# The last 320 columns of wo group 4 in fifteen short transfers instead of with the rest

## The chip, the cores and the metric

The kernel runs on one core of a Trainium2 chip. The metric is device time in microseconds (us) of one execution; three executions of the kernel before gave 526.68, 526.82 and 527.18 us, so its time is 526.82 us, the median. The core has five engines that work side by side and meet through semaphores: PE (TensorE, matmuls), DVE (VectorE), ACT (ScalarE), POOL (GpSimd) and SP (SyncE). Here SP does nothing but issue DMA transfers, and 16 DMA engines move what it issues.

## The reference: what is computed

Four tokens (batch 4, one position each, D = 640) are normalised, and two branches are added to them: attention over a cache, and a gated feed-forward layer.

```python
W = min(4096, max(256, Sk // 4))                 # 2048 of the 8192 cached positions
q = (xn @ wq).reshape(4, 1, 32, 192)             # 32 heads of 192
scores = einsum("bhqd,bhkd->bhqk", q, k[:, :, Sk - W:]) * 192 ** -0.5
p = softmax(scores)
o = einsum("bhqk,bhkd->bhqd", p, v[:, :, Sk - W:])
return x + o.reshape(4, 1, 6144) @ wo + (silu(xn @ w1) * (xn @ w3)) @ w2
```

Every head has keys and values of its own, so each element of the windows of K and V is used for one token only. Of the 222.96 MB that are read, nearly all is K and V: 32 heads with two tensors of 3 MB each.

## The kernel before

**Tiling.** A head's K window, 4 tokens by 2048 positions by 192, lies in SBUF as 128 partitions by 64 positions by 192 (24,576 bytes in each partition); V lies in the same way. There are two K buffers (`kt`) and two V buffers (`vt`). The vector `q` is spread over all partitions (`qbc`).

**One head.** DVE multiplies K by q in two halves (`mult`, L275, 128x6144 each). For each half PE adds the products in groups through an identity matrix (`adder`, L373, 12 matmuls), and DVE reduces what is left (`reduce_half`, L281). Then comes the softmax: a maximum (L286), a transpose on PE (`tr`, L431), a second maximum (L290), ACT's scaling (L352), PE's broadcast (`bc`, L435), ACT's exponential (L356) and the masked weights `z` (L295). PE multiplies them with V (`pv`, L448). Two heads share a normalisation (`osum`, L456, and L299, L304); a transpose (L307) makes `oT`, one for each group of four heads.

**The output projection.** `wo` has 6144 rows, taken as eight groups of 768 rows (`hg` 0 to 7). A group lies as 128 partitions by 6 rows by 640, so 3840 elements, or 7680 bytes, in a partition. The matmuls of a group (`proj`, L385) run late: groups 0 to 4 among the last heads, and groups 5 to 7 behind the last head.

**The order of SP's queue** is written out by hand. First come wq, w1, w3 and w2; then for each head `load_k` and `load_v`. `load_k(h+2)` waits until DVE's reduction has shown that the K buffer is free (`s_red`, L158), and `load_v` until PE has finished with the V buffer (`s_pv`, L164). The w1, w3 and w2 tiles (`wts[0]` to `wts[2]`) are free early, and three issues at L188 put wo into them: groups 0 and 1 at h = 4, groups 2 and 3 at h = 6, and group 4 alone at h = 8, each after `load_k(h+2)` and `load_v(h+1)`. All three count up one semaphore, `s_wom`, by 16 each. PE waits for 48 on it (L498) ahead of `proj(0)`. Groups 5, 6 and 7 go into a K buffer at the very end (L196, L198, L199).

**Parts that matter for the change:** `wo_of(hg)` and `wo_src(hg)` (L145 to L151) give a group's place in SBUF and its source, both with 128 rows of 3840 elements; SP's loop (L180 to L189); and PE's wait (L498).

Of the kernel before, what the change touches and what calls it, by code (L numbers as in the profile page):

```python
# [16 lines left out]
def kernel(  # L17
# [14 lines left out]
    P = 128  # L32
    B, Sq, D = A_x.shape
# [16 lines left out]
    QW = HG * Dh  # L50
    RPP = QW // P
    N0 = D // 2
    QC = 512
    NQ = H * Dh // QC
    FW = F // HG
    NP = H // 2
    assert D % P == 0 and F % QC == 0 and P % B == 0 and W % (PB * GQ) == 0
    assert JQ * DD == 512 and JQ % 2 == 0 and 2 * Dh + 2 <= 512 and 2 * N0 == D and N0 <= 512
    assert NQ == 12 and KC == 5 and QW % P == 0 and Dh == CT * RPP and P == HG * CT and F == HG * CT * FC
# [11 lines left out]
    def sb(name, shape, dt):  # L71
        return ctx.enter_context(nc.sbuf_tensor(name, shape, dt))
# [9 lines left out]
    wts = [sb(f"wt{i}", [P, KC * F], BF16) for i in range(3)]  # L82
# [62 lines left out]
    def wo_of(hg):  # L145
        t = wts[hg // 2][:, :] if hg < 5 else wo_end
        i = hg % 2 if hg < 5 else hg - 5
        return t[:, i * RPP * D:(i + 1) * RPP * D]

    def wo_src(hg):  # L150
        return A_wo[hg * QW:(hg + 1) * QW, :].rearrange("(p i) n -> p (i n)", i=RPP)  # L151


    sp = nc.sync

    def load_k(h):
        if h >= 2:
            sp.wait_ge(s_red, 2 * (h - 2) + 1)  # L158
        sp.dma_start(out=flat(kt[h % 2]), in_=k_win[:, h].rearrange("b (p j) d -> p b (j d)", p=PB)).then_inc(s_k[h % 2], 16)

    def load_v(h, j0=0, j1=NJ, s=None):
        if j0 == 0:
            if h >= 2:
                sp.wait_ge(s_pv, h - 1)  # L164
            else:
                sp.wait_ge(s_pp, 13)
        sp.dma_start(out=vt[h % 2][:, j0:j1, :].rearrange("q j d -> q (j d)"),
                     in_=v_win[:, h].rearrange("b (p j) d -> p b j d", p=PB)[:, :, j0:j1, :].rearrange("p b j d -> p b (j d)")
                     ).then_inc(s or s_v[h % 2], 16)
# [10 lines left out]
    for h in range(H - 2):  # L180
        load_k(h + 2)
        if h < H - 4:
            load_v(h + 1)
        if h in (4, 6, 8):
            g = h - 4
            n = 2 if g < 4 else 1
            sp.wait_ge(s_pp, 16)
            sp.dma_start(out=wts[g // 2][:, 0:n * RPP * D].rearrange("p (g i) -> p g i", g=n),  # L188
                         in_=A_wo[g * QW:(g + n) * QW, :].rearrange("(g p i) n -> p g (i n)", g=n, i=RPP)).then_inc(s_wom, 16)  # L189
    load_v(H - 3)  # L190
    load_v(H - 2)
    load_v(H - 1, 0, NJ // 2)
# [38 lines left out]
    def dv(fn, *a, own=True, **k):  # L231
        if n_dv[0] and own:
            ve.wait_ge(s_dv, n_dv[0])
        fn(*a, **k).then_inc(s_dv, 1)  # L234
        n_dv[0] += 1
        return n_dv[0]
# [22 lines left out]
    for c0 in (0, 6):  # L259
        for i in (1, 3, 5):  # L260
            ve.wait_ge(s_pp, 1 + c0 + i + 1)
            n = dv(ve.tensor_copy, out=qbc[:, (c0 + i) * QC:(c0 + i + 1) * QC], in_=q_banks[i], own=False)
# [35 lines left out]
    def norm_rec():  # L298
        ve.reciprocal(out=rt[:], in_=mt[:, P + 1:P + 2]).then_inc(s_rec, 1)  # L299

    def norm_og(i):
        sl = slice(i % 2 * 2 * CT, (i % 2 + 1) * 2 * CT)
        ve.wait_ge(s_sum, 2 * i + 2)
        ve.tensor_scalar_mul(out=og[sl].rearrange("p i r -> p (i r)"), in0=po[sl, 0:Dh], scalar1=rt[sl, 0:1]).then_inc(s_og, 1)  # L304
        if i % 2:
            ve.wait_ge(s_og, i + 1)
            ve.transpose(out=oT[:, i // 2].rearrange("p i r -> p (i r)"), in_=flat(og)).then_inc(s_oT, 1)  # L307
# [23 lines left out]
    norm_rec()  # L331
    ve.wait_ge(s_rec, NP)
    norm_og(NP - 1)
    ve.wait_ge(s_acc, 1)  # L334
# [35 lines left out]
    pe = nc.tensor  # L370
# [67 lines left out]
    def tot():  # L438
        for par in range(2):
            m = pe.matmul(mt[:, P + 1:P + 2], lhsT=flat(tot_w[:, par]), rhs=rsum[par][:], start=(par == 0), stop=(par == 1))  # L440
        return m
# [35 lines left out]
    pe.addr_align(256, max_nops=8)  # L477
    with pe.While(lambda: pe.snap(cnt) < NP - 1):
        for par in range(2):
# [15 lines left out]
    adder(1)  # L495
    take(pe, s_z)
    tot()
    pe.wait_ge(s_wom, 48)  # L498
    pe.wait_ge(s_oT, 5)
    proj(0)  # L500
    pv(1)
# [60 lines left out]
```

## Time and profile before

| | |
|---|---|
| three runs | 526.68, 526.82, 527.18 us |
| the profiled execution's own time | 526.78 us |
| its span, first to last instruction | 524.9 us |
| busy PE, DVE, ACT | 366.4, 334.6, 54.1 us |
| mean granted TensorE clock | 0.857 |
| moved by DMA | 223.07 MB, mean 425 GB/s |
| issues of K | 32 of 3072 KB, median 19.6 us from issue to landing |
| issues of V | 31 of 3072 KB, 22.5 us; 2 of 1536 KB, 10.8 us |
| issues of wo into `wts` | 2 of 1920 KB, 28.6 us; 1 of 960 KB (group 4), 29.1 us |

The page divides the span into 40 slices of 13.1 us and gives for each one the busy share of every engine, the granted clock and the traffic. The trace behind it can be asked for the instructions of a stretch in order of time, for who waited for whom, and for the packets that the DMA engines moved. A packet record has its queue, start, duration and size; queue q1 is SP's, q10 is ACT's, and the two queues of the kind "instruction" fetch the engines' programs.

### The profile page before, as it was taken

The page shows a single profiled execution, that of the slowest core. Times are in us where ns is not written, and L with a number is a line of the kernel's source. Part 1 is how long each engine was busy: PE and PEld are TensorE (multiplying, and loading weights), DVE is VectorE, ACT ScalarE, POOL GpSimd, SP SyncE. Part 2 cuts the span into 40 slices and gives each one's busy share as a digit, 9 for nine tenths or more (in the row PEclk, how much of TensorE's full clock was granted, in tenths as well). Part 3 has the DMA queues.
Part 4 walks back from the last instruction along what each step waited for, and adds up shares of the span by engine and source line. Part 5 has one row for each costly group of instructions (what it writes and reads, how often), then busy time and mean ns, then how long its engine had stood idle before and what let it go on. Part 6 is the DMA issues. An engine that isn't in the chain of part 4 may idle for free. (4 is left out here: it accounts for less than half of the span.)

```text
span 524.9 us, 4774 instructions
## 1 busy us (share of the span) xinstructions
PE 366.4 (70%) x2306; PEld 83.7 (16%) x1553; DVE 334.6 (64%) x287; ACT 54.1 (10%) x174; POOL 3.4 (1%) x16
## 2 busy tenths in 40 slices
PE   2775777667586367876667666887676767587897
PEld 0010111111211011121111111111111112111133
DVE  3136777767267564678767676667776666666871
ACT  2120101101101011011101111110110011111010
POOL 2000000000000000000000000000000000000000
PEclk9887888878869788788878888888797888888799
DMA  8999999999999999999999999999999999999995
GB/s 356 423 441 429 428 436 426 442 421 427 443 429 436 427 427 444 429 431 438 425 440 425 438 429 433 434 429 438 425 442 423 440 429 431 438 425 440 425 424 231
DMA packets 11520, 223.07 MB, mean 425 GB/s; under 512 B 1260, under 2 KB 1400, under 8 KB 2424
## 3 DMA queue, kind: packets, MB, share of 16 engines
q1 hardware_dynamic: 11496, 222.96, 98.9%
q8 instruction: 4, 0.07, 0.0%
q14 instruction: 4, 0.03, 0.0%
q10 hardware_dynamic: 16, 0.01, 0.0%
HBM read 222.96 MB, written 0.01 MB: 425 GB/s over the span
## 5 line engine op out<-in xcount | busy, mean ns | idle before, releaser
L373 PE MATMUL ps<-prs,idb 128*128 128x512 bf16 x768 | 229.0, 461 | 134.1 <-PEq L136 134.1
L275 DVE TENSOR_TENSOR prs<-kt,qbc 128x6144 bf16<-128x6144 bf16 x64 | 214.5, 3353 | 120.1 <-DMA kt<-in_A_k_cache_dram 120.1
L281 DVE TENSOR_REDUCE sc<-ps 128x32 f32<-128x1024 f32 x64 | 77.5, 1211 | 3.3 <-PE ps L373 3.1
L456 PE MATMUL po<-o_sb,sel_w 128*128 128x192 f32 x128 | 49.0, 516 | 0.7 <-PEq L136 0.7
L448 PE MATMUL o_ps<-vt,z 128*8 128x384 bf16 x1024 | 47.2, 326 | 0.1
L352 ACT ACTIVATE gneg<-gmax 1x128 f32<-1x128 f32 x32 | 9.8, 308 | 290.1 <-DVE gmax L290 290.1
L448 PEld LDWEIGHTS o_ps<-vt,z 128*8 128x8 bf16 x1024 | 22.1, 86 | 54.6 <-issue 42.0
L422 PEld LDWEIGHTS <-idb 128*128 128x128 bf16 x64 | 6.3, 98 | 153.1 <-issue 152.6
L456 PEld LDWEIGHTS po<-o_sb,sel_w 128*128 128x128 f32 x128 | 25.3, 221 | 14.7 <-issue 5.2
L359 ACT COPY o_sb<-o_ps 128x384 f32<-128x384 f32 x32 | 15.3, 479 | 117.4 <-PE o_ps L448 117.4
L295 DVE TENSOR_TENSOR z<-ex,mask_b 128x256 bf16<-128x256 bf16 x32 | 13.6, 424 | 18.9 <-ACT ex L356 18.4
L431 PEld LDWEIGHTS mt<-idf,lmax 128*1 128x1 f32 x32 | 3.3, 104 | 118.9 <-issue 118.9
L290 DVE TENSOR_REDUCE gmax<-mt 1x4 f32<-1x128 f32 x32 | 8.8, 276 | 10.6 <-PE mt L431 10.1
L440 PEld LDWEIGHTS mt<-rsum,tot_w 128*128 128x128 f32 x64 | 9.6, 191 | 35.1 <-issue 34.7
L234 DVE CAST qbc<-ps 128x512 bf16<-128x512 f32 x4 | 2.6, 686 | 19.7 <-PE ps L373 19.7
L435 PE MATMUL mt<-one,gneg 1*128 1x1 f32 x64 | 11.9, 253 | 4.0 <-PEq L136 3.8
L373 PE MATMUL ps<-vt,xnT 128*128 128x512 bf16 x31 | 10.6, 477 | 5.0 <-DMA vt<-in_A_wq_dram 3.9
L435 PEld LDWEIGHTS mt<-one,gneg 1*128 1x128 f32 x64 | 9.4, 182 | 22.4 <-issue 22.4
L356 ACT ACTIVATE ex<-sc,negm 128x64 bf16<-128x64 f32 x32 | 11.1, 348 | 1.0
L431 PE MATMUL mt<-idf,lmax 128*1 128x128 f32 x32 | 10.5, 328 | 0.0
L304 DVE TENSOR_SCALAR og<-po,rt 64x192 bf16<-64x192 f32 x16 | 6.6, 414 | 3.8 <-PE po L456 3.6
L440 PE MATMUL mt<-rsum,tot_w 128*128 128x1 f32 x64 | 8.1, 231 | 0.0
(65 smaller groups left out, 79.6 us busy)
## 6 DMA issues: line engine op xcount, KB each, us to landing
kt<-in_A_k_cache_dram SPq DMA_DIRECT2D x32, 3072.0 KB, 19.6
vt<-in_A_v_cache_dram SPq DMA_DIRECT2D x31, 3072.0 KB, 22.5
vt<-in_A_wq_dram SPq DMA_DIRECT2D x2, 3072.0 KB, 13.2
wt<-in_B_w_dram SPq DMA_DIRECT2D x3, 1920.0 KB, 27.8
wt<-in_A_wo_dram SPq DMA_DIRECT2D x2, 1920.0 KB, 28.6
vt<-in_A_v_cache_dram SPq DMA_DIRECT2D x2, 1536.0 KB, 10.8
kt<-in_A_wo_dram SPq DMA_DIRECT2D x2, 960.0 KB, 14.6
prs<-in_A_wq_dram SPq DMA_DIRECT2D x1, 1536.0 KB, 19.9
```

What stands on the lines that cost most here:

```text
L275: ve.tensor_tensor(out=prs[:, a].rearrange("p q j d -> p (q j) d"), in0=kt[h % 2][:, 2 * a * JQ:2 * (a + 1) * JQ, :], in1=qbc[:, h * Dh:(h ...
L281: ve.tensor_reduce(out=sc[h % 3][:, 2 * a * JQ:2 * (a + 1) * JQ], in_=ps[:, a].rearrange("p q (j d) -> p (q j) d", d=DD), axis=AX.X, op=AL ...
L295: ve.tensor_tensor(out=z[h % 2][:], in0=ex[h % 2][:].unsqueeze(2).to_broadcast([P, NJ, B]), in1=mask_b[:].unsqueeze(1).to_broadcast([P, NJ ...
L352: ae.mul(out=gneg[h % 2][:], in_=gmax[h % 2][:].unsqueeze(1).to_broadcast([1, PB, B]), mul=-SCALE).then_inc(s_gneg, 1)
L356: ae.activation(out=ex[h % 2][:], in_=sc[h % 3][:], func=ACTF.Exp, bias=negm[h % 2][:, 0:1], scale=SCALE, accum_out=rsum[h % 2][:]).then_i ...
L359: ae.copy(out=o_sb[h % 2][:], in_=o_ps[:, 0:2 * Dh]).then_inc(s_osb, 1)
L373: return pe.add_instruction(mybir.InstMatmult(name=nc.get_next_instruction_name(), engine=pe.engine, ins=[pe.lower_ap(rhs), pe.lower_ap(lh ...
L431: pe.transpose(out=mt[0:1, 0:P], in_=lmax[par][:], identity=idf[:]).then_inc(s_tr, 1)
L435: pe.matmul(mt[:, P:P + 1], lhsT=flat(gneg[par]), rhs=one[:], start=True, stop=True).then_inc(s_bc, 1)
L440: m = pe.matmul(mt[:, P + 1:P + 2], lhsT=flat(tot_w[:, par]), rhs=rsum[par][:], start=(par == 0), stop=(par == 1))
L448: m = pe.matmul(o_ps[c * CT:c * CT + 2 * B, 0:2 * Dh].rearrange("p (a d) -> p a d", a=2), lhsT=z[par][:, 2 * jj:2 * jj + 2, :], rhs=vt[par ...
L456: m = pe.matmul(po[:, 0:Dh], lhsT=flat(sel_w[:, par, k]), rhs=o_sb[par][:, k * Dh:(k + 1) * Dh].rearrange("p (r i) -> p i r", i=RPP), star ...
```

## The change

The transfers of groups 0 to 3 stay as they are. Group 4's transfer of 128 rows by 3840 elements becomes one of 128 rows by the first 3520 elements (7040 bytes a row), and after it 15 transfers of the last 320 elements (640 bytes a row): rows 0 to 14, then rows 15 to 28, and so on with 13, 12, ..., 2 rows, and 9 rows at the end (together 128). Each adds 16 to `s_wom`, and PE waits for 48 + 16 x 15 = 288 in place of 48. The bytes and their places are the same.

```diff
+    CUTS = [*range(15, 1, -1), 9]
+    assert sum(CUTS) == P
...
             sp.wait_ge(s_pp, 16)
-            sp.dma_start(out=wts[g // 2][:, 0:n * RPP * D].rearrange("p (g i) -> p g i", g=n),
-                         in_=A_wo[g * QW:(g + n) * QW, :].rearrange("(g p i) n -> p g (i n)", g=n, i=RPP)).then_inc(s_wom, 16)
+            if n == 2:
+                sp.dma_start(out=wts[g // 2][:, 0:n * RPP * D].rearrange("p (g i) -> p g i", g=n),
+                             in_=A_wo[g * QW:(g + n) * QW, :].rearrange("(g p i) n -> p g (i n)", g=n, i=RPP)).then_inc(s_wom, 16)
+            else:
+                c1 = RPP * D - N0
+                sp.dma_start(out=wo_of(g)[:, 0:c1], in_=wo_src(g)[:, 0:c1]).then_inc(s_wom, 16)
+                r0 = 0
+                for r in CUTS:
+                    sp.dma_start(out=wo_of(g)[r0:r0 + r, c1:], in_=wo_src(g)[r0:r0 + r, c1:]).then_inc(s_wom, 16)
+                    r0 += r
...
-    pe.wait_ge(s_wom, 48)
+    pe.wait_ge(s_wom, 48 + 16 * len(CUTS))
```

## The prediction

> **What bounds the kernel now.** I read the page's slices and queues first, then the waits of the last 45 us, then the instructions of that stretch in order of time, and last the packet records.
>
> The page, slices and queues:
>
> ```profile
> DVE  3136777767267564678767676667776666666871
> DMA  8999999999999999999999999999999999999995
> GB/s 356 423 441 429 428 436 426 442 421 427 443 429 436 427 427 444 429 431 438 425 440 425 438 429 433 434 429 438 425 442 423 440 429 431 438 425 440 425 424 231
> q1 hardware_dynamic: 11496, 222.96, 98.9%
> q8 instruction: 4, 0.07, 0.0%
> q14 instruction: 4, 0.03, 0.0%
> ```
>
> The DMA engines are full in every slice but the first and the last, while DVE has idle time throughout. Nearly all packets are SP's (q1). The waits from 480 us on:
>
> ```profile
> DVE prs L275 <- DMA kt<-in_A_k_cache_dram: 3.9, 1, 3.9
> ```
>
> and the instructions of that stretch:
>
> ```profile
> 484.65 3.36 DVE L275 TENSOR_TENSOR prs<-kt,qbc 128x6144 bf16<-128x6144 bf16 x1 [3.90 <-DMA kt<-in_A_k_cache_dram]
> 488.15 5.28 PE L373 MATMUL ps<-prs,idb 128*128 128x512 bf16 x12 [4.43 <-PEq L136]
> ...
> 496.33 3.35 DVE L275 TENSOR_TENSOR prs<-kt,qbc 128x6144 bf16<-128x6144 bf16 x1
> ```
>
> At 484.65 DVE has waited 3.9 us for the K of head 30. From there to the end engines hand work to each other without a long wait for data: head 30's products, their sums on PE (5.28 us, at half clock), head 31's products at 496.33, and the tail. The chain of waits ends so:
>
> ```profile
> 517.54 0.04 issue
> 517.59 1.58 PE po L456 x4
> 519.17 2.56 PE acc L385 x36
> ```
>
> The end is therefore the landing of head 30's K (484.62) plus 40.3 us of tail. One other landing is as late: head 29's V at 499.15, when PE reaches it at 499.26. Both move with the DMA engines. So the question is what the change does to **the slowest DMA engine**, because a transfer has landed when the last of its engines is done.
>
> The packet records give that engine by engine. On q1 each packet starts 3 or 4 ns before another ends; linking them so gives 16 unbroken chains of 718 packets, one per DMA engine, up to the end of wo. No chain ever idles; each runs at the same rate, and they are apart only by their start and by instruction fetches: a 16,384-byte packet on q8 costs the engine that carries it 0.86 to 0.95 us, an 8192-byte one on q14 0.31 us. When K 30 ends, the last engine (call it **A**; two fetches, at 89.3 and 324.4) is at 0, the next (**B**; a fetch at 60.5) 0.03 us ahead, the third 0.61 ahead, and all 13 others 1.35 to 1.98 us ahead. The number of an engine isn't recorded.
>
> **The change, part by part.**
>
> *SP's issues.* The stretch on SP (issue times and durations):
>
> ```profile
> 171.29 0.54 SPq L167 DMA_DIRECT2D vt<-in_A_v_cache_dram  x1
> 171.87 0.59 SPq L188 DMA_DIRECT2D wt<-in_A_wo_dram  x1
> 186.22 0.54 SPq L159 DMA_DIRECT2D kt<-in_A_k_cache_dram  x1
> 190.38 0.54 SPq L167 DMA_DIRECT2D vt<-in_A_v_cache_dram  x1
> ```
>
> Fifteen issues are added behind the one at 171.87, so SP's K load of head 11 and V load of head 10 (186.22 and 190.38) stand behind them. A small one isn't shown; the nearest rows are the 4-row output issues (0.28 on ACT, 0.35 on SP), the longest load issue took 0.65. So 15 x (0.28 to 0.65) = 4.2 to 9.8 us, and 15 gaps of 0.05, from 172.46: done between 177.4 and 183.0. The nearest rows are the 4-row ones, so I take 6 us. K's load isn't allowed before 186.22, so at least 3.2 of the 13.8 us stay free: cost nothing. If that cover went, the queue would still hold work until group 4 lands at 171.87 + 29.1 = 200.95; an issue takes 1.04 us to its first packet (0.96 to 1.995 at the start), so only past about 199.9 would the engines run dry.
>
> *PE's wait* for 288 instead of 48 costs nothing: what it counts has landed near 201, and the wait stands at 498, with `proj(0)`, `pv` and all later PE work behind it.
>
> *The packets.* A row of 7680 bytes takes 291 ns, one of 6400 takes 244, one of 1280 takes 55 (the last wo transfers), and a semaphore packet 9. The slope is (244 - 55) / 5120 = 0.0369 ns a byte. So 7040 bytes take 268 ns; 640 bytes take 31 by the slope, and 35 in SP's output packets. Each starts 4 ns before the one ahead has ended. Before, an engine had 8 rows: 8 x 287 = 2296 ns. After, 8 x 264 = 2112, and for each short row that it gets 31 + 5 = 36 ns (27 + 5 = 32 by the slope): **-184 + 32n to 36n ns**, n being its short rows. The break-even is at 5 to 6 rows, below the mean of 8, because each short row brings a semaphore packet.
>
> *How n is spread.* The page's small packets count the engines that take part: SP's 78 loads leave 16 semaphore packets each (1248) and its 4-row output leaves 4; ACT's two 4-row transfers leave 16 packets on q10, 4 data and 4 semaphore each, with overlapping data packets (starts 1.854 to 1.949, up to 0.16 long). A 4-row transfer uses 4 engines, one row each. I take it that r rows use r engines. Then an engine gets 0 to 15 short rows whichever they are, and bounds for A or B are -0.18 us (n = 0) and +0.36 (n = 15). Where always the same first r engines serve, n falls along them as 15, 15, 14, 13, 12, 11, 10, 9, 8, 6, 5, 4, 3, 2, 1, 0. Ten of the sixteen values (6 and more) are a loss, and the loss of either A or B is enough: over all pairs of places for the two, the later one moves by -0.08 to +0.33 us in nine cases of ten, in the middle by +0.19 (34 ns a row). The order in which the chains start (A fifth, B fourteenth) would give A n = 12, +0.2 to +0.25, but start order is weak evidence, and B's n = 2 would not help. I take **+0.2 us**.
>
> [...]
>
> *Overhead of many transfers.* The row that bears on it is the last wo piece (160 KB, L199): a transfer of its own right behind another, its packets abut, and it landed 0.40 us after the one before it (520.29 to 520.69), which is 8 x 51 ns and no fixed time on top. So I charge none. [...]
>
> *Sum:* SP 0, PE 0, packets +0.2 on the last engine, passed on unchanged to K 30, V 29 and the tail: 526.78 + 0.2 = 526.98. The profiled execution is 0.04 under the median, so I say 527.0.
>
> **The rivals.**
>
> *1. The last engines are relieved.* A and B both get 0 to 4 short rows: -0.18 to -0.04 us, 526.6 to 526.8. For it: it needs only that A and B lie at the light end. Against: only five of the sixteen places are so light, and two engines must both lie there, 5 x 4 of 16 x 15 pairs, 1 in 12.
>
> *2. SP is held up by transfers in flight* (the slower side). At 180 us five large transfers and 15 small ones would be outstanding, 20; the trace shows 8 at most (5.4 us, before the first landing at 10.81). If the queue takes 16, the last small issues wait for landings up to 198.65, and K's load for head 11 goes out about when group 4 lands at 200.95: issue 0.54 + 1.04 of bubble on all engines, +1.5 us, 528.3. If it takes 8, three small ones go at once and four with those landings; eight would still be unissued at 200.95, 8 x 0.4 more, about +4.7 us, 531.5. It decides from a limit below 20. Against it: packets outstanding per engine are no more than the trace has (4 x 9 + 30 = 66 after the landing at 176.84, against about 69 at 5.4 us).
>
> *3. Short packets stall an engine,* each pair of row and semaphore waiting for its receipt. The receipt is 0.33 us (the last engine ends at 520.37, its landing is 520.69): 8 to 15 rows give 2.6 to 5 us, less the lead of the engine that has them (0 to 1.98): +1 to +5 us, 528 to 532. Likewise if all 128 rows went to one engine: 128 x 0.034 - 0.18 = 4.2, less its lead, 529 to 531. Against: after each of 1252 semaphore packets the next row starts at once.
>
> *4. The clock moves.* The half-clock stretch at 486.9 to 493.7 doubles the sums at 488.15 (5.28 us; 2.76 at full clock). A shift that moves it off gives -2.5 us (524.3), a second one on the tail costs as much. Against: three runs lie within 0.5 us.
>
> **How the numbers follow.** About 0.2%, 1.05 us, is what a measurement of this kernel can tell from no change. My case (+0.05 to +0.36) 0.66; rival 1 and nothing (-0.18 to +0.05) 0.18; rival 2 0.05, rival 3 0.04; rival 4 0.07, 0.04 of it faster and 0.03 slower. So faster 0.04, slower 0.12, within 0.84. The packets' bounds around the median, -0.18 to +0.36, go from 526.64 to 527.18; with the runs' scatter (-0.14 and +0.36) they go from 526.5 to 527.54. I set 526.5 to 527.6, which leaves out rivals 2 to 4, 0.16 together.
>
> **What would show it.** q1 should have 256 packets more (128 rows, 128 semaphore packets), 11,752. SP's 15 short issues should end before 183 and K's load stay at about 186.2. In each chain the piece for group 4 should change by -184 + 32n to 36n ns, the n being the falling list, and K 30 should land 0.05 to 0.36 us later. An idle gap in a chain after 200 us would make rivals 2 or 3 right, and A and B at the light end rival 1. Another instruction fetch (SP's program is longer) on A or B would add 0.31 us that I haven't counted.

## The result, and the profile after

| | before | after |
|---|---|---|
| median, runs made side by side | 526.84 us (7 runs, 526.66 to 527.89) | 529.06 us (7 runs, 528.55 to 530.06) |
| ratio, 95% interval | | 1.0036, 1.0023 to 1.0049 |
| the profiled execution, its span | 526.78, 524.9 us | 528.67, 526.8 us |
| mean granted TensorE clock | 0.857 | 0.853 |

The kernel is 2.2 us (0.36%) slower, outside the predicted range (to 527.6). Between the two profiled executions the difference is 1.89 us, and that is what the traces have to explain. Some executions of kernels met below took 550 to 576 us, with K and V transfers of some 8.1 us for a long stretch; the comparisons and the medians given here leave them out, and the profile of after2, which is of one of them (565.87 us), isn't read.

The page after, slices and queues:

```profile
DMA  8999999999999999999999999999999999999995
GB/s 357 424 440 422 442 421 441 424 442 417 442 431 433 431 424 414 440 425 440 425 440 425 440 425 439 425 439 427 435 431 435 429 437 429 433 431 425 440 389 224
q1 hardware_dynamic: 11752, 222.96, 98.8%
q8 instruction: 4, 0.07, 0.0%
```

q1 has the 256 packets more that were predicted. The DMA engines stay full in every slice but the first and the last, as before. Two slices stand out in the traffic: the sixteenth (197 to 211 us; 414, it was 444) is where the short rows move, and the 39th (500 to 514; 389, it was 424) is the tail. The page alone thus says that two places lost time, 300 us apart, and that neither shows as idle engines in its DMA row.

SP's issues after (start, duration, what was issued):

```profile
172.17 0.59 SPq L195 DMA_DIRECT2D wt<-in_A_wo_dram  x1
172.80 5.41 SPq L198 DMA_DIRECT2D wt<-in_A_wo_dram  x15
186.70 0.54 SPq L161 DMA_DIRECT2D kt<-in_A_k_cache_dram  x1
```

The 15 issues end at 178.2, and K's load of head 11 goes out at 186.70, when its buffer is free. This step held, and rival 2 is out.

Now the landing of head 30's K, and the end, in order of time:

```profile
486.06 3.36 DVE L285 TENSOR_TENSOR prs<-kt,qbc 128x6144 bf16<-128x6144 bf16 x1 [3.94 <-DMA kt<-in_A_k_cache_dram]
...
522.62 0.98 PE L395 MATMUL acc<-kt,oT 128*4 128x320 bf16 x12 [0.28 <-DMA kt<-in_A_wo_dram]
```

The products of head 30 start at 486.06; they started at 484.65. So **1.41 us** are lost up to there, and 1.90 - 1.41 = 0.49 us behind. The second line is new: PE waits 0.28 us for a piece of wo at the very end. The chain of waits after has it too:

```profile
500.73 1.50 PE o_ps L458 x32
502.23 0.01 issue
502.25 0.53 SPq L169
...
504.59 17.89 DMA kt<-in_A_wo_dram
522.48 0.14 issue
522.62 1.00 PE acc L395 x12
```

The end was set by PE's `po` and `acc`; now it is set by transfers, from `pv` of head 29 (which frees the V buffer for V 31) through SP's issues to wo's landing.

The bandwidth of two stretches, by windows. The columns are the stretch, its length, the busy time of PE, PE's loads, DVE, ACT and POOL, then the granted clock, the DMA share and GB/s. Before:

```profile
198.00:205.00 7.00, 7.00 (x29) 1.93 (x12) 3.40 (x4) 0.91 (x4) 0.00 (x0) 0.84 1.04 445
505.00:510.00 5.00, 4.96 (x58) 1.61 (x47) 2.88 (x5) 1.06 (x4) 0.00 (x0) 1.00 1.00 424
```

and after:

```profile
198.00:205.00 7.00, 7.00 (x57) 2.43 (x44) 3.35 (x4) 0.91 (x4) 0.00 (x0) 1.00 1.07 415
505.00:510.00 5.00, 4.88 (x35) 1.20 (x26) 3.31 (x6) 0.91 (x4) 0.00 (x0) 1.00 0.95 356
```

In the seven microseconds after 198 the engines move 30 GB/s less, and the DMA share (1.07) says that they are as busy as ever. **The engines are not idle there; their packets are longer.** In the tail both go down (0.95, 356): there engines do run dry.

**Where the 1.41 us come from.** The packet records, linked into one chain for each engine as in the prediction, give A's packets around its short rows (bytes, count, ns each):

```
7040 x8     267
640 x13      32   each with a semaphore packet of 9
24576        1581     K of head 11, first packet   (before: 912)
24576        1412     second packet                (before: 912)
24576 x6     912
```

The short rows themselves cost what was predicted, 32 ns, and so do the 7040-byte rows. But **the two large packets behind them take 1.17 us longer**. From the end of V 9 to the end of K 11, A took 9.57 us before and 11.00 after: +1.43, where -184 + 34 x 13 gives +0.26. Over the 16 engines, eight lost 0.99 to 1.70 us and eight between -0.18 and +0.19. The sum is 10.5 us of engine time, where the formula's sum is 16 x (-0.184) + 128 x 0.034 = 1.4. (The small packets can't always be linked to one engine without doubt; the sums and the large packets don't depend on it.)

When V 9 ends, A is 0.84 us ahead of B after (0.81 before). With +1.43 it becomes the last engine, 0.73 behind B, and K 11's packets end 0.63 us later (-0.84 + 1.43, and 0.04 that the transfers ahead were late). At 324 us A's second instruction fetch comes. In the trace of before it costs 0.84 us and not 0.31: the packet (309 ns) and 0.53 more in the 24,576-byte packet behind it (1445 in place of 912). Before, this was covered by A's lead but for 0.03; after, nothing covers it: K 30 would end 0.63 + 0.84 - 0.03 = 1.44 us later; its packets end 1.43 later. By landings, which the rest of the text uses, it is 0.66 at K 11 and 1.41 at K 30. DVE's wait for K 11 shows the first of these, before and after:

```profile
208.30 3.36 DVE L275 TENSOR_TENSOR prs<-kt,qbc 128x6144 bf16<-128x6144 bf16 x1 [5.13 <-DMA kt<-in_A_k_cache_dram]
208.96 3.36 DVE L285 TENSOR_TENSOR prs<-kt,qbc 128x6144 bf16<-128x6144 bf16 x1 [6.82 <-DMA kt<-in_A_k_cache_dram]
```

A's loss repeats: linked in the same way, A takes 1.44 us more than before from V 9 to K 11 in the executions of after_v31 and after_wo5, two kernels of the next section with the same transfers up to there.

**The 0.49 us behind.** wo's last piece lands 36.86 us after K 30 (36.07 before). The loss lies in V 31's two half transfers, whose 12,288-byte packets take 0.5 to 0.7 us in place of 0.46 between 505 and 510, while the engines furthest ahead (by up to 3.16 us at K 30, it was 1.98) run dry for 0.07 to 0.35 us at 505.

### The profile page after: what moved, and what is told of

The parts are those of the page before. It is cut to its first block, busy times and chain, and to the rows that moved or that the text cites. A ratio compares the mean times of both kernels' runs of the same rounds, so it can differ in the third digit from the quotient of the medians.

```text
span 526.8 us, 4789 instructions
## 1 busy us (share of the span) xinstructions
PE 366.3 (70%) x2306; PEld 82.9 (16%) x1553; DVE 334.4 (63%) x287; ACT 54.3 (10%) x174; POOL 3.4 (1%) x16
## 3 DMA queue, kind: packets, MB, share of 16 engines
q1 hardware_dynamic: 11752, 222.96, 98.8%
```

## The experiments

The first theory after the result was that a run of short packets starves the large packets behind it. The runs turned it into another: **transfers with fewer than 128 rows, one right behind another, cost the engines more than their packets show, and large packets of other transfers pay the difference.** Rivals: it is the number of small packets or of semaphores; it is the number of transfers; it is the neighbouring partitions that the rows of one transfer write to; or it is A's ranking alone, with the rest a coincidence. The first kernels vary the number of rows per transfer, the others take one suspect each. In the table, "K 11" is the interval between the landings of K 10 and K 11 against the 16.87 us of before, and "K 30" its landing against 484.62 (one profiled execution each). Ratio and interval are against before, run beside it.

| kernel | transfers of group 4 | median us | ratio (95%) | K 11 | K 30 |
|---|---|---|---|---|---|
| after | 128 x 3520, then 15 of 15 ... 9 rows x 320 | 529.06 | 1.0036 (1.0023 to 1.0049) | +0.62 | +1.41 |
| even8 | 128 x 3520, 8 of 16 x 320 | 527.74 | 1.0012 (1.0003 to 1.0021) | +0.64 | +0.76 |
| even8step | the same, each of every eighth row | 527.49 | 1.0013 (1.0004 to 1.0022) | +0.74 | +0.61 |
| even16 | 128 x 3200, 16 of 16 x 320 | 528.94 | 1.0038 (1.0026 to 1.0050) | +1.85 | +2.07 |
| one128 | 128 x 3520, 128 x 320 | 527.12 | 1.0003 (0.9990 to 1.0017) | +0.01 | +0.21 |
| cols8 | 8 of 128 x 480 | 527.19 | 1.0008 (0.9999 to 1.0016) | +0.32 | +0.71 |
| rows112 | 112 and 16 whole rows | 530.10 | 1.0067 (1.0053 to 1.0080) | +2.75 | +3.03 |
| rows64 | 64 and 64 whole rows | 531.00 | 1.0086 (1.0073 to 1.0099) | +4.12 | +4.22 |
| rows16 | 8 of 16 whole rows | 531.68 | 1.0099 (1.0080 to 1.0117) | +3.76 | +3.68 |
| rows16step | the same, each of every eighth row | 531.15 | 1.0081 (1.0065 to 1.0098) | +4.14 | +3.95 |
| rows3 | 112 whole rows, then 3, 3, 3, 3, 3, 1 | 530.51 | 1.0078 (1.0065 to 1.0091) | +3.36 | +3.07 |
| spread | after's transfers, 15 of them one by one behind later loads | 527.85 | 1.0020 (1.0010 to 1.0029) | -0.21 | not read |
| spread2 | the same | 528.05 | 1.0020 (1.0011 to 1.0030) | -0.20 | +0.59 |
| after_wo5 | after's | 529.46 | 1.0045 (1.0028 to 1.0063) | +0.92 | +1.58 |
| after_v31 | after's | 528.30 | 1.0023 (1.0014 to 1.0032) | +1.08 | +1.44 |
| after2 | after's | 528.96 | 1.0033 (1.0021 to 1.0046) | not read | not read |

### even8: the same bytes, evenly spread

```diff
-    CUTS = [*range(15, 1, -1), 9]
+    CUTS = [16] * 8
```

> The short columns come in 8 transfers of 16 rows, so every DMA engine gets 8 short rows and nobody more. The trace after shows that the short packets themselves cost what was predicted (up to 0.51 us for 15), but that the first one or two 24,576-byte packets behind 9 or more of them take 1.05 to 1.86 us in place of 0.91. Theory (a run of short packets leaves the engine without data for the large packets behind it, from about 9 short rows on): 8 rows stay under it, each engine loses 0.09 to 0.2 us, head 30's K lands at about 484.8, time 526.9 to 527.1. Rival (uneven load alone is what costs): no unevenness, 526.9. Rival (each added transfer costs, however it is spread): half of the change's loss or more, 528 and up.

Half a miss, and the more useful for it: K 11 comes 0.64 us late, with eight rows on every engine, where the formula gives 8 x 34 - 184 = +0.09 us. The windows of this kernel show the same fall as after's:

```profile
198.00:205.00 7.00, 7.00 (x49) 2.29 (x36) 3.47 (x4) 0.91 (x4) 0.00 (x0) 0.97 1.05 416
```

So it isn't the uneven spread that costs: eight rows take 0.64 + 0.18 = 0.82 us by the landing, 0.103 us a row; by the sum over the 16 engines (8.2 us) it is (8.2 + 16 x 0.184) / 128 = 0.087. In after, (10.5 + 16 x 0.184) / 128 = 0.105. These are means: in after, the eight engines that lost little show that the price isn't the same for every row. But with all engines moved alike, A stays ahead of B by what it was, its fetch at 325 stays covered, and nothing is added from K 11's landing (209.06, +0.78) to K 30's (+0.76), against 0.75 in after (+0.66 and +1.41). That separates the two terms: some 0.65 us for few rows, 0.75 for a fetch laid open by the unevenness.

### even16: twice the short rows

```diff
+                for c in (c1, c1 + N0):
+                    r0 = 0
+                    for r in CUTS:
+                        sp.dma_start(out=wo_of(g)[r0:r0 + r, c:c + N0], in_=wo_src(g)[r0:r0 + r, c:c + N0]).then_inc(s_wom, 16)
+                        r0 += r
```

with `c1 = RPP * D - 2 * N0` and `CUTS = [16] * 8`.

> The last 640 columns come in two column blocks, each in 8 transfers of 16 rows: every engine gets 16 short rows in one run. By the packets alone each engine changes by 8 x (244 - 291) + 16 x 34 = +0.17 us. Theory (starved large packets behind a long run): 1.2 to 1.5 us more on every engine alike, head 30's K lands 1.4 to 1.7 us later than before, time 528.2 to 528.7, although no engine has more to do than another. Rival (uneven load alone): 527.0.

+1.85 us. The 6400-byte rows save 8 x (291 - 244) = 0.38, so 16 rows cost 2.23 us, 0.14 each: the cost grows somewhat faster than the count. The first K packet behind them takes 0.83 to 1.2 us longer on all engines, the second 0.26 to 0.74.

### one128: the same short rows in one transfer

```diff
-    CUTS = [*range(15, 1, -1), 9]
+    CUTS = [P]
```

> The last 320 columns come in one transfer of 128 rows, 8 short rows on every engine with one semaphore packet. Theory W (engines that write into neighbouring partitions at the same moment hinder one another; a transfer of all 128 rows spreads the engines, one of 16 neighbouring rows does not): no large packet behind the short ones is stretched, each engine changes by -184 + 8 x 27 + 5 = +0.04 us, time 527.0 as before. Theory S (a run of short packets starves the large ones behind it): 8 short rows and 1 semaphore packet, at most what 8 transfers of 16 rows cost, K of head 11 up to 0.65 us later, up to 527.6.

The eight short rows of each engine are the same packets as in even8, with one semaphore packet in place of eight. The loss is gone (+0.01), and no packet behind them is stretched:

```profile
198.00:205.00 7.00, 7.00 (x43) 2.32 (x32) 3.61 (x4) 0.91 (x4) 0.00 (x0) 0.89 1.05 448
```

So it isn't the short rows as such. Open between the count of transfers, their semaphores, and their few rows. (In its profiled execution, 528.78, wo's last piece landed 1.4 us later behind K 30 than before, with long packets in V 31 as in after; the median of its 11 runs is 527.12.)

### cols8: eight transfers, each of 128 rows

```diff
+                w = RPP * D // 8
+                for i in range(8):
+                    sp.dma_start(out=wo_of(g)[:, i * w:(i + 1) * w], in_=wo_src(g)[:, i * w:(i + 1) * w]).then_inc(s_wom, 16)
```

> Group 4 comes in 8 transfers of all 128 rows by 480 columns: 64 packets of 960 bytes and 8 semaphore packets on every engine, in one run of 72. Theory F (what is slow is any transfer that does not have all 128 rows: then the DMA engines no longer each write to the partitions that they serve in a 128-row transfer, and rows move at 155 to 165 GB/s in place of 425): none of that, 64 x 39 + 8 x 5 - 2301 = +0.24 us by the slope of the packets, head 11's K 0.2 to 0.3 us later, time 527.1 to 527.3. Theory S (a run of many short packets starves what follows): 72 packets are more than in the change or in the 16 short rows, so 1.4 us or more, 528.4 and up. Theory N (each transfer's semaphore packet holds an engine up): 8 transfers, as many as of 16 whole rows, K of head 11 about 3.7 us later, 531.

As many transfers and semaphores as in even8, and 64 short packets (960 bytes, 44 ns) per engine in place of 8. From the packets: 64 x (44 - 4) + 8 x 5 - 2296 = +0.30 us; measured +0.32, with no stretched packet. Thus **neither the count of transfers, nor of semaphores, nor of small packets** makes the loss:

```profile
198.00:205.00 7.00, 7.00 (x50) 2.29 (x36) 3.76 (x4) 0.91 (x4) 0.00 (x0) 0.99 1.07 441
```

SP's queue in this kernel shows something else:

```profile
173.92 17.76 SPq L196 DMA_DIRECT2D wt<-in_A_wo_dram  x8
191.73 4.59 SPq L161 DMA_DIRECT2D kt<-in_A_k_cache_dram  x1
```

Eight issues take 17.76 us and K's issue 4.59: here SP is held up, which rival 2 expected; by what, no run shows. It costs nothing: K's load has gone out by 196.32, before the work queued ahead of it is done (group 4 landed at about 201 in before), and the +0.32 at K 11 is within 0.02 of what the packets give.

### rows112 and rows64: whole rows, two transfers

```diff
-                c1 = RPP * D - N0
-                sp.dma_start(out=wo_of(g)[:, 0:c1], in_=wo_src(g)[:, 0:c1]).then_inc(s_wom, 16)
...
+                    sp.dma_start(out=wo_of(g)[r0:r0 + r], in_=wo_src(g)[r0:r0 + r]).then_inc(s_wom, 16)
```

with `CUTS = [112, 16]` and `[64, 64]`.

> Group 4's whole rows come in two transfers, of 112 and of 16 rows: every engine has 7 + 1 packets of 7680 bytes as before and one semaphore packet more. Theory F: 983,040 bytes at 155 to 165 GB/s in place of 425, 5.9 to 6.3 us in place of 2.3, head 11's K 3 to 4 us later, time 530 to 531. Theory N (semaphore packets): one more, 527.0 to 527.3. Theory S: no short packets, 527.0. If the loss of the kernel with 112 rows and six transfers of 3 and 1 rows came from those six, this one shows little of it.

> Group 4's whole rows come in two transfers of 64 neighbouring rows, 4 + 4 packets on every engine. Theory F, if it holds for every number of rows but 128: head 11's K 3 to 4 us later, 530 to 531. If the loss needs 16 engines in 16 neighbouring rows, 64 rows spread over 16 engines lose less, 0.5 to 2 us, 527.5 to 529. Theories N and S: 527.0.

These have no small data packet at all and one transfer more than before. They lose 2.75 and 4.12 us, on a group whose 983,040 bytes take 2.3 us at 425 GB/s. If the whole loss is put on the group, it moves at 983,040 / (2.3 + 2.75) = 195 and 983,040 / (2.3 + 4.12) = 153 GB/s. In rows64:

```profile
198.00:205.00 7.00, 7.00 (x54) 2.74 (x44) 3.33 (x4) 0.91 (x4) 0.00 (x0) 0.89 1.01 236
```

The DMA share is 1.01 while the traffic is 236 GB/s. Together with one128 and cols8 this is the cleanest pair of the study: two transfers of 128 rows cost nothing, two of 64 rows cost 4.12 us. The wait of rows64 for K 11:

```profile
212.45 3.36 DVE L283 TENSOR_TENSOR prs<-kt,qbc 128x6144 bf16<-128x6144 bf16 x1 [10.33 <-DMA kt<-in_A_k_cache_dram]
```

The packet records show something more. Five packets of V 9, which every engine has *ahead* of group 4, take 0.95 to 2.55 us in place of 0.91: they begin between 196.30 and 197.93, on engines that are still at V 9 while others have begun with group 4 at 196.46. V 9 lands at 201.27 (198.65 before), and at 199.76 in rows112. So it isn't only the packets behind an engine's own rows that pay.

### rows16, rows16step and even8step: neighbouring rows or every eighth

rows16 is `CUTS = [16] * 8` with whole rows, as above. The two others take row j, j + 8, j + 16 and so on:

```diff
+                for j in range(len(CUTS)):
+                    sp.dma_start(out=wo_of(g)[j:P:8, c1:], in_=wo_src(g)[j:P:8, c1:]).then_inc(s_wom, 16)
```

(even8step; rows16step without the columns.)

> No short rows at all: group 4's 128 whole rows of 7680 bytes come in 8 transfers of 16 neighbouring rows, so every engine has the same 8 packets as before and 7 semaphore packets more (0.04 us). [...] Theory S: no short packets, 527.0.

> The 8 transfers of 16 whole rows again, but of every eighth row. Theory W: the rows of a transfer lie over the whole of SBUF; at most half of the loss of the neighbouring rows is left, K of head 11 0 to 2.5 us later, time 527.0 to 529.3. Theory S: no short packets, 527.0. If the loss is as large as with neighbouring rows, it is not the place in SBUF but the number of transfers with 16 rows.

> As the 8 transfers of 16 rows, but each takes every eighth row (j, j+8, ..., j+120) instead of 16 neighbouring ones. The packets of every engine are the same in number, size and order; only the partitions differ. Theory W: most of the 0.65 us by which head 11's K came later is gone, 0.05 to 0.3 us is left, time 527.0 to 527.3. Theory S (number of short packets): the same 0.65 us, 527.7.

+3.76 against +4.14, and +0.64 against +0.74 (even8): the strided forms are no better. That the rows of one transfer are neighbours is not the cause. In rows16 most of the 7680-byte packets are 300 to 450 ns longer than 291, and the first two K packets behind them 0.7 and 0.46 us.

### rows3: fewer rows for some engines

```diff
-    CUTS = [*range(15, 1, -1), 9]
+    CUTS = [3, 3, 3, 3, 3, 1]
...
+                sp.dma_start(out=wo_of(g)[0:P - 16], in_=wo_src(g)[0:P - 16]).then_inc(s_wom, 16)
+                r0 = P - 16
```

and whole rows in the loop.

> No short columns: group 4's first 112 rows come in one transfer (7 rows an engine, one less than before), and its last 16 whole rows of 7680 bytes in transfers of 3, 3, 3, 3, 3 and 1 rows, on the first three engines if the first engines serve. Theory (few and long packets starve nothing): 13 engines, with those that fetch DVE's and most of PE's program among them, change by 5 - 292 = -0.29 us, the first three by +1.2 to +1.5, which they were ahead, but for the one that fetches ACT's program (1.31 ahead): head 30's K lands 0.15 to 0.29 earlier, time 526.5 to 526.7, at worst 526.9. Rival (any transfer of few rows starves what is behind it): the first three engines lose 2.2 us or more and K lands 0.3 to 0.9 later, 527.1 to 527.7.

A miss. I had looked for a gain, by giving the late engines less to do. It lost 3.36 us, and on all 16 engines alike: most of the 7680-byte packets took 0.11 to 0.3 us more and the next K packets 0.9, 0.85 and 0.19. rows112 puts most of it down to what both have in common: there 112 rows and one transfer of 16 already cost 2.75. How much the 112 rows cost by themselves no run shows.

### spread and spread2: the short transfers one by one

```diff
+    left = []
+
+    def one_short():
+        if left:
+            g, r0, r, c1 = left.pop(0)
+            sp.dma_start(out=wo_of(g)[r0:r0 + r, c1:], in_=wo_src(g)[r0:r0 + r, c1:]).then_inc(s_wom, 16)
...
-                    sp.dma_start(out=wo_of(g)[r0:r0 + r, c1:], in_=wo_src(g)[r0:r0 + r, c1:]).then_inc(s_wom, 16)
+                    left.append((g, r0, r, c1))
```

`one_short()` stands behind each `load_k` and `load_v` of the loop.

> The same 15 transfers of 15, 14, ..., 2 and 9 rows, but one behind each of the following K and V loads, so the same rows and bytes on the same engines, and never more than one short row in a run. Theory (starved packets behind a long run): no large packet is stretched; the engine that also fetches DVE's program has 13 rows, 13 x 34 - 184 = +0.26 us, and is the last one, so head 30's K lands 0.26 later and the time is 527.1. Rival (unevenness of bytes and rows alone): as after the change, 529.

> The kernel with the 15 short transfers one by one behind later loads, once more. Its first profiled execution had three slow K and V transfers from 288 to 313 us (8.1 us each in place of 7.25), where only one more short transfer was on its way. If that belongs to the short transfers, it is there again and the profiled time is above 529; if it was a disturbance, head 19's K lands 0.1 to 0.3 us later than before (324.7 to 324.9), and the undisturbed time is 527.0 to 527.4.

K 11 is early by the saved bytes (-0.21 and -0.20; -0.18 predicted for n = 0), and the ratio, 1.0020 twice, is better than after's. But by the median it isn't the +0.26 us of the packets: spread2 is 1.03 us above the 527.02 beside it. In its profiled execution, 527.54, K 30 is 0.59 late, with +0.17 between K 11 and K 19 and +0.62 between K 19 and K 20, across A's fetch.

The chains of that execution say where the 0.59 comes from. A's lead over the last engine is 0.586 us when V 9 ends, and 0.483, 0.347 and 0.213 at the ends of K 13, K 15 and K 17. By the list of n, A has by then 3, 7 and 11 short rows more than the last engine, and at 34 ns a row that makes 0.10, 0.24 and 0.37 us, which is what is seen. No 24,576-byte packet between V 9 and 480 us takes more than 966 ns, apart from the two behind fetches. So **a single transfer of few rows between large ones cost its packets and nothing more here**; the costly ones come one right behind another. The 0.59 is then A's lead, which was 0.23 smaller than before ahead of all short rows, the 0.26 of the packets, 0.08 more behind the fetch (1528 ns in place of 1445) and 0.04 at 272 us, where one packet of every engine was that much longer, 0.61 in all. Why the median lies another 0.5 us higher is open.

spread's own profile (531.68 us) was no good measure of this. From 288 to 312 us three K and V transfers took 8.1 to 8.2 us each in place of 7.25:

```profile
288.00:312.00 24.00, 18.20 (x123) 4.50 (x85) 13.49 (x14) 2.77 (x10) 0.00 (x0) 0.86 1.01 389
```

With 1020 to 1052 ns for nearly every 24,576-byte packet, on all 16 engines. spread2, the same program, has no such stretch.

### after_wo5: a filling for the hole at 505

```diff
+    sp.wait_ge(s_red, 2 * (H - 2) + 1)
+    sp.dma_start(out=wo_of(5), in_=wo_src(5)).then_inc(s_wo5, 16)
     load_v(H - 1, 0, NJ // 2)
     load_v(H - 1, NJ // 2, NJ, s_v31)
```

> The changed kernel with one transfer moved: wo group 5 (960 KB) is issued ahead of head 31's two V transfers instead of behind them. In the changed kernel the engines that are 1.8 to 3.1 us ahead run out of work at 505, because head 31's V may only be issued when PE has done head 29 (502.25), and then 504 to 510 is slow (12,288-byte packets of 0.5 to 0.7 us in place of 0.46). Theory: 2.3 us of cover close that hole; wo's last piece lands 34.8 to 36.2 us after head 30's K (36.1 before, 36.9 in the changed kernel), the chain at the end is one of compute again, and the time is 0.3 to 0.6 us less than the changed kernel's, 528.1 to 528.7. Rival (the loss of the last 20 us belongs to the instruction fetches at 504 and 516 and not to the hole): no gain, 528.6 to 529.1, and the long packets stay.

A miss. With group 5 ahead of V 31 the engines have work at 505:

```profile
505.00:510.00 5.00, 4.89 (x32) 1.27 (x23) 3.31 (x6) 0.91 (x4) 0.00 (x0) 1.00 0.98 404
```

The traffic there is 404 in place of 356, but V 31's long 12,288-byte packets stay, wo's last piece still lands 36.91 us after K 30, and V 31 itself lands at 514.83 in place of 512.29. The time is 529.46, not below after's. So closing the hole doesn't bring wo's last piece forward. It isn't a clean test of the time: V 31 now stands behind group 5, and the end comes 42.6 us after K 30 (40.8 in after), with `po` and `acc` of PE last in the chain.

### after_v31: V 31 in one transfer

```diff
-    load_v(H - 1, 0, NJ // 2)
-    load_v(H - 1, NJ // 2, NJ, s_v31)
+    load_v(H - 1)
...
-    pv(1, 0, NJ // 2)
-    pe.wait_ge(s_v31, 16)
-    pv(1, NJ // 2, NJ)
+    pv(1)
```

> The changed kernel with head 31's V in one transfer of 24,576-byte rows instead of two of 12,288. Theory H (the slow stretch from 505 to 510 comes from two half-row transfers in flight with engines 3 us apart): gone, wo's last piece lands 36.0 to 36.3 us after head 30's K, 0.3 to 0.6 us less time than the changed kernel. Rival (engines that run dry and start together, whatever the transfer): packets of 24,576 bytes over 0.95 us between 505 and 510, and 36.6 to 37 us.

K 30 is 1.44 late as in after, but from there to the end it takes 40.35 us, as before (40.3); after takes 40.8. wo's last piece lands 36.26 us after K 30 (36.86), and the chain ends in compute again:

```profile
519.05 1.58 PE po L465 x4
520.63 2.56 PE acc L394 x36
```

So **the tail's 0.49 us belong to V 31's two half transfers**. It is the best version that keeps the short transfers together, 528.30 against 529.06. Why the halves suffer is open. That the engines are far apart at K 30 doesn't decide it: the first is 1.95 us ahead of the last in rows16 and 2.0 in one128, and 61 of V 31's 256 packets take over 0.5 us in each; it is 2.25 in even8 and 2.1 in rows64, and none and one do. The kernel before with V 31 in one transfer wasn't run.

### after2: the change once more

The kernel is after's, unchanged.

> The changed kernel once more, as it is. Of its loss, 1.41 us is there when head 30's K lands; 0.47 us of the span is added behind that, where 12,288-byte packets of head 31's V took 0.5 to 0.7 us instead of 0.46 between 505 and 510. If that is a lasting part, wo's last piece lands 36.9 us after head 30's K again (36.1 before). If it is a disturbance of one execution, it lands 36.0 to 36.2 after it, the span is about 526.3, and the loss of 1.4 us at head 30's K stands alone.

528.96 us and 1.0033: the size of the loss holds. Whether the tail's part of it lasts, which was the question, no profile answers; that the median is 0.66 above after_v31's beside it speaks for it. For the first part the executions of after_wo5 and after_v31 stand in, with the same transfers up to there: K 30 is +1.58 and +1.44 late, after's +1.41, though how much of it is there in the interval up to K 11 differs (+0.92, +1.08, +0.62). A's own loss is the same in all three (1.43 and twice 1.44); in after_v31 another engine is the last one at K 11, 0.46 behind A.

No version beat the kernel before.

## Why the prediction was wrong

**The step that failed: "The packets".** It priced a short row by its own packet record, 31 + 5 ns, and the trace after has that very duration. But the price isn't in that record. Where transfers of few rows followed one another, a row cost 0.105 us of an engine's time on the mean in after (0.087 in even8), three times as much, and 0.07 of it shows up as longer 24,576-byte packets behind it. So A lost 1.43 us, not the +0.26 that its n gives. It would have needed a trace in which transfers of few rows run *behind a full queue and ahead of large packets*. The 4-row transfers of before run at the start and the end, not in a full queue. And the row on which "Overhead of many transfers" rested, the last wo piece, is a transfer of 128 rows. It was right for those (one128 +0.01, cols8 as computed) and said nothing of others. I took it across a change of shape without naming that as a choice.

**The second term: the fetch, and the ranking of the engines.** The prediction charged 0.31 us for an 8192-byte fetch, from the packet alone; with the packet behind it, it is 0.84. And it ranked the engines by their ends at K 30, "A at 0, B 0.03 ahead". That hid that at 200 us, where the change acts, A was 0.81 ahead of B and would spend just this lead on its fetch at 324. What was late next was thus read at the wrong time. The 0.75 us between K 11 and K 30 come from here; even8, with all engines alike, adds nothing there. (In after_v31's execution only 0.26 is added there, because at K 11 another engine is still behind A.)

**The third: "passed on unchanged to K 30, V 29 and the tail".** The tail grew by 0.49 us in the profiled execution, in V 31's half transfers, whose packets got longer; after_v31, without the halves, has the old tail. What makes them longer isn't known, so whether the tail of this change could have been foreseen stays open.

The sum: 0.66 at K 11's landing + 0.75 up to K 30's + 0.49 behind = 1.90 us, the difference of the spans (526.8 - 524.9).

**What held.** SP's issues and K's load cost nothing (the issues end at 178.2, the load goes out at 186.70); PE's wait cost nothing (the last 640-byte packet starts at 200.51, `proj(0)` at 499.67); 256 packets more (11,752 on q1, it was 11,496); the 7040-byte and 640-byte packets' own durations (267 and 32 ns); the half-clock stretch of rival 4 stayed, with the sums of head 30 at 5.28 us again (granted clock 0.50 from 489.6 to 494.8). No chain is idle between 200 and 482 us; at 482.61 three chains pause for up to 0.50 us, which came too late to matter for K 30, since K 20 was 1.43 us late already. One instruction fetch on q14 moved from 506.75 to 401.95; between K 20 (+1.43) and K 30 (+1.41) it added nothing on the last engine. The list of n held as well: A's and the last engine's steps in spread2 are those of its fourth and fifteenth place.

**The rivals.** Rival 1 (the last engines relieved) would have needed A among the lightest; it was among the eight that lost. Rival 3 had the right side and the right size (+1 to +5 us) at a chance of 0.04, but another mechanism: not each pair of row and semaphore waits (they abut, and cols8 and one128 show that semaphores and short packets cost only their records), but transfers of few rows right behind one another do cost more, and packets of other transfers pay. Its argument against, "after each of 1252 semaphore packets the next row starts at once", was true and no defence: the two large packets behind A's rows took 1.17 us longer without any gap.

**What stays open.** Why transfers of fewer than 128 rows are slow when they follow one another. V 9's long packets in rows64 (up to 2.55 us in place of 0.91) point to engines that hinder one another rather than to an engine's own order of work. The records don't say which partitions an engine writes, so the mechanisms of theories W and F, which turn on that, are not shown by any run. What the runs show is the loss by shape, at K 11: +0.01 and +0.32 for transfers of 128 rows (one128, cols8), +2.75 as 112 and 16 whole rows, +4.12 as 64 and 64, +3.76 as 16 neighbours eight times and +4.14 as every eighth row. It doesn't grow steadily as a transfer's rows get fewer.

## What to carry to other kernels

Cut a transfer by columns that keep all 128 rows, not by rows: two pieces of 128 rows cost nothing here (one128, +0.01 us at K 11), two of 64 rows cost 4.12 us on 0.98 MB (rows64). Where rows have to be cut, single small transfers between large ones cost less here than a run of them: spread2's median is 1.03 us above before's, after's 2.2. A packet's duration is not its price (32 ns against 0.105 us for a short row of after); look at the packets around it as well, and at the traffic of the stretch, since a full DMA share hid a fall from 445 to 236 GB/s here (shares of 1.04 in before and 1.01 in rows64). Where the slowest of several engines decides, rank them at the time of the change, and then follow each one's later costs that its lead had covered.

## What the runs showed of the hardware

- Transfers of fewer than 128 rows, one right behind another, were slow with 7680-byte and with 640-byte packets: 153 GB/s for whole rows as 64 and 64, 195 as 112 and 16 (estimates from the landing of K 11), and 0.09 to 0.10 us on the mean for a row of 640 bytes whose packet takes 32 ns (even8, after). Single ones between large transfers cost 34 ns a row (spread2).
- Packets ahead of such rows were slowed as well, on other engines: V 9 in rows64, up to 2.55 us in place of 0.91.
- An instruction fetch cost a DMA engine more than its packet: 8192 bytes 0.84 us on A (309 ns, and 533 in the next packet) and 0.55 to 0.58 on the engines with the fetches at 138 us of before and 402 of after (309, and 242 to 276), 16,384 bytes 1.43 (949, and 481, at 60 us of before).
- SP was held up while it issued in cols8: eight transfers of 128 rows (64 rows on an engine) took it 17.76 us, and the next one 4.59. In after 15 transfers with at most 15 short rows on an engine were issued in 5.41 us. What held it up no run shows.
- All 16 engines ran at a second, lower rate for a stretch of spread's profiled execution: 1020 to 1052 ns in place of 912 for a 24,576-byte packet at 389 GB/s, over 24 us. What starts and ends it is open.
- Half transfers late in the queue (V 31) were slower in some executions, 0.5 to 0.7 us a packet in place of 0.46 (after, one128, rows16), and not in others (before, even8, rows64). The distance between the engines at K 30 doesn't tell which.
